# Delta-rule attention and expert layer in one kernel: the second block's norms moved beside tick 0, nineteen inverse steps in ticks 0 to 7, and v's scaling split between ScalarE and VectorE

## The chip, the cores and the metric

The kernel runs on one core of one Trainium2 chip. The metric is device time in microseconds of one execution. Where a trace is quoted, it is of one profiled execution, and times in it count from that execution's first instruction. The engines are named as the profile names them: PE is TensorE (PEld its weight loads), DVE is VectorE, ACT is ScalarE, POOL is GpSimd, SP is the engine that issues most DMAs.

## What is computed

```python
batch, n_heads, seq, head_dim = (4, 8, 768, 48)
k_n = k / (np.linalg.norm(k, axis=-1, keepdims=True) + 1e-06)
state = np.zeros((B, H, D, D))
for t in range(S):
    y[:, :, t] = einsum('bhd,bhde->bhe', q[:, :, t], state)
    v_old = einsum('bhde,bhd->bhe', state, kt)
    state = state + bt[:, :, :, None] * einsum('bhd,bhe->bhde', kt, vt - v_old)
...
x = y.transpose(0, 2, 1, 3).reshape(3072, 384)
# then 8 experts, top 1 by x @ w_gate: out = gate * (relu(x @ w1[e]) @ w2[e])
```

The first part is a recurrence over 768 tokens for 32 pairs of batch and head. The second part sends each of 3072 tokens through one of eight expert networks.

## The kernel before

**Blocks, sub-blocks and ticks.** The 768 tokens are cut into six blocks (`tb`) of 128, and each block into four sub-blocks of 32 tokens. A pair of block and batch has a number n = 4 tb + b, from 0 to 23. The recurrence runs as a pipeline of 27 ticks: in tick t, sub-block q of pair n = t − q is treated for q = 0 to 3, and q sits on partitions 32q to 32q + 31. So a tick works on 128 partitions, and each block takes four more ticks.

**What one tick does, in the order of the code.** `residual(t)` multiplies the keys with the state and with earlier results on PE (the `ks` matmuls of L392 and L404) and subtracts that from the scaled v on DVE (L411, `v_all<-v_all,ks`). `apply(t)` multiplies with the inverse on PE (L419, `ks<-v_all,wt`), and ACT copies the four results out (L423, `u<-ks`). PE can't start L419 of a tick before DVE's L411 of that tick, and DVE can't start L411 before the `ks` matmuls of that tick. Besides, each tick holds a part of `kpart` (transposed keys, and their Gram matrices: matmuls `pg`, ACT copies `gg`, L244), of `qpart` (matmuls `pq`, ACT copies `pm`), of `finish` (state update `st`, output `yp`, router logits) and of `emit_slots`. PE's matmuls `pt`, `qt`, `pg` and `pq` share one ring of three PSUM buffers, six tiles a tick, so that the second half of `pq` takes the buffer that the first `gg` copy frees.

**Norms and inverses of a block.** For each block DVE has two long jobs. `prepare(tb)` finds the norms of the keys from the diagonals of the Gram matrices (`ss<-lg` is its first instruction, then a square root on ACT at L302, then ten short instructions, and the transposes into `nt_all`). `lanes(tb)` inverts 32x32 triangular matrices column by column: 31 columns, each a product (`tmp`, L353) and a difference (`lw`, L360), one generator step each, and at the end a transpose into `wt` (L366), which `apply` uses. The Gram diagonals reach `prepare` through DRAM: when the fourth pair of a block has its `gg` copies, SP issues four writes `gd<-gg` and one read `lg<-gd` (L248, L251). This happens in ticks 2, 6, 10 and 14 for blocks 2 to 5, and before tick 0 for block 1.

**Order.** All instructions of the recurrence stand on each engine in the order of the code. `inverses(steps, t)` takes steps of `prepare` or `lanes` of the next block from a queue, and `beside(t, i)` calls it at seven places of each tick with `STEPS = (3, 3, 3, 2, 2, 2, 2)`, 17 steps a tick. `scale_v(t + 1)` multiplies the next tick's v with the norms, one DVE instruction (L375, 128 x 384). Before tick 0, the kernel runs `prepare(0)`, `scale_v(0)`, 56 steps of `lanes(0)`, all of `prepare(1)` and the rest of `lanes(0)`.

**Experts.** From tick 20 on, weights are loaded and split into two parts, and after tick 26 the experts run, bound by PE.

Of the kernel before, what the change touches and what calls it, by code (L numbers as in the profile page):

```python
# [12 lines left out]
AF = mybir.ActivationFunctionType  # L13
# [5 lines left out]
B, H, S, D = 4, 8, 768, 48  # L19
C = 128  # L20
NT = S // C
# [19 lines left out]
def deltanet_moe(ctx, tc, q, k, v, beta, w_gate, w1, w2, out):  # L41
    nc = tc.nc
# [62 lines left out]
    LAG = NB - 1  # L105
# [2 lines left out]
            -4, -1, 'l')  # L108

    STEPS = (3, 3, 3, 2, 2, 2, 2)  # L110
    W1 = 4
    DM2 = 0
    DEF = 2
# [35 lines left out]
    nt_t = lp.tile([128, (NT * B + LAG) * H], F32, name="nt_all")  # L149
# [38 lines left out]
    def rows(t):  # L188

        if t < NB:  # L190
            return [slice(0, 32 * (t + 1))]
        return {NT * B: [slice(32, 64), slice(64, 128)], NT * B + 1: [slice(64, 128)],
                NT * B + 2: [slice(96, 128)]}.get(t, [slice(0, 128)])
# [91 lines left out]
    def prepare(tb):  # L285

        T = tiles[tb]
        if tb == 0:
            T["lg"] = fp.tile([128, 32, 32], F32, name="lg0", tag="lg", bufs=2)
        lg = T["lg"]  # L290
        lw = T["lw"]
        ss, s0, r0 = (lp.tile([128, 32], F32, name=f"{n_}{tb}", tag=n_) for n_ in ("ss", "s0", "r0"))
        if tb == 0:
            nc.vector.transpose(out=ss, in_=sst)
            yield
            nc.vector.tensor_scalar(out=ss, in0=ss, scalar1=1e-36, scalar2=None, op0=ALU.max)
        else:
            nc.vector.tensor_scalar(out=ss, in0=lg.rearrange("p a b -> p (a b)")[:, 0:1024:33],
                                    scalar1=1e-36, scalar2=None, op0=ALU.max)
        for _ in range(6 if tb > 1 else 1):  # L300
            yield
        nc.scalar.activation(out=s0, in_=ss, func=AF.Sqrt)  # L302
        yield
        nc.vector.reciprocal(r0, s0)
        yield
        nc.vector.tensor_tensor(out=r0, in0=r0, in1=ss, op=ALU.mult)
        yield
        nc.vector.tensor_tensor(out=s0, in0=s0, in1=r0, op=ALU.add)
        yield
        nc.vector.tensor_scalar(out=s0, in0=s0, scalar1=0.5, scalar2=1e-6, op0=ALU.mult, op1=ALU.add)  # L310
        yield
        nc.vector.reciprocal(r0, s0)
        yield
        nc.vector.tensor_tensor(out=ss, in0=r0, in1=bl[:, tb, :], op=ALU.mult)
        yield
        nc.vector.tensor_tensor(out=lw.rearrange("p a b -> p (a b)")[:, 0:1024:33], in0=ss, in1=r0, op=ALU.mult)
        yield
        nc.vector.tensor_tensor(out=r0, in0=ss, in1=r0, op=ALU.mult)
        yield
        if tb == 0:  # L320
            nc.vector.transpose(out=lg, in_=tiles["dg"].rearrange("p h t -> p t h"))
            yield
        nc.vector.tensor_tensor(out=lg, in0=lg, in1=r0.unsqueeze(2).broadcast_to([128, 32, 32]), op=ALU.mult)
        for q in range(NB):
            p = slice(32 * q, 32 * q + 32)
            nc.vector.transpose(out=nt_t[p, (B * tb + q) * H:(B * tb + q) * H + 32], in_=s0[p])
            yield
        T["nt"] = True
# [39 lines left out]
            clear_w(tb + 2)  # L368
        yield

    def scale_v(t):

        vn = vt[t]
        for r in rows(t):
            nc.vector.tensor_tensor(out=vn[r], in0=vn[r], in1=nt_t[r, t * H:(t + 1) * H].unsqueeze(2)  # L375
                                    .broadcast_to([r.stop - r.start, H, D]), op=ALU.mult)

    def clear_u(n):
        us[n] = lp.tile([128, H * D], F32, name=f"u{n}", tag="u", bufs=UB)

        nc.sync.dma_start(out=us[n][32:128], in_=zrow[32:128, 0:H * D])
# [31 lines left out]
    def apply(t):  # L413

        ks, vn = tiles["ks", t], vt[t]
        for h in range(H):
            for q, n in stage(t):
                r = slice(32 * q, 32 * q + 32)
                nc.tensor.matmul(ks[r, h, :], lhsT=tiles[n // B]["wt"][r, n % B * H + h, :], rhs=vn[r, h, :],  # L419
                                 start=True, stop=True, tile_position=(32 * q, 32 * q), skip_group_check=True)  # L420
        for i, (q, n) in enumerate(reversed(stage(t))):
            r = slice(32 * q, 32 * q + 32)
            nc.scalar.copy(out=uview(n)[r], in_=ks[r])  # L423
            if i == 2:
                yield

    def finish(n):
# [29 lines left out]
        yield  # L457
        w = 1 if n >= NN - W1 else 2
        if n % w == 0:
# [97 lines left out]
    def run(gen, steps=1):  # L557

        for _ in range(steps):
            if next(gen, tiles) is tiles:  # L560
                return False
        return True

    def chunk(q, t=-1):

        while q and q[0][0] <= t:
            if run(q[0][1]):
                return
            q.pop(0)
# [154 lines left out]
    NN = NT * B  # L724
# [12 lines left out]
    for i in range(NB):  # L737
        nc.sync.dma_start(out=bl[32 * i:32 * i + 32],
                            in_=beta.rearrange("b h (t i s) -> i (b h) t s", t=NT, i=NB)[i])
# [8 lines left out]
    lane = prepare(0)  # L748
# [15 lines left out]
    slots += [xt[e * CAP + NG * 128:e * CAP + NG * 128 + 64, :].unsqueeze(1) for e in range(E)]  # L764
    while "nt" not in tiles[0]:
        run(lane)
    scale_v(0)
    clear_u(0)
    qs0 = {n: qs_[n][1] for n in range(NN)}
    ks0 = {n: ks_[n][1] for n in range(NN)}  # L770
# [5 lines left out]
    ks_ = [x for i, x in enumerate(ks_) if f"k{i}" not in done]  # L776
    qs_ = [x for i, x in enumerate(qs_) if f"q{i}" not in done]
    lane = lanes(0)
    run(lane, 56)
    run(prepare(1), 100)  # L780
    run(lane, 100)
    queue = [(tb, lanes(tb)) for tb in range(1, NT)]
    before = [(tb, prepare(tb)) for tb in range(2, NT)]
    W = None

    def inverses(steps, t):

        while steps > 0 and queue:
            tb, lane = queue[0]
            if t < B * (tb - 1) and "cols" not in tiles[tb - 1] or ("cols" in tiles[tb] and t < B * tb - 1):  # L790
                break
            if before and before[0][0] == tb:
                if run(before[0][1]):
                    steps -= 1
                else:
                    before.pop(0)
            elif run(lane):
                steps -= 1
            else:
                queue.pop(0)  # L800
# [4 lines left out]
    def ahead_step():  # L805
        if order and not (order[0] == "o" and len(last) < DEF):
            run(other if order.pop(0) in "to" else ahead)

    def beside(t, i):

        inverses(STEPS[i], t)
        if before and (t, i) >= (B * before[0][0] - 5, 3):
            if not run(before[0][1], 3):
                before.pop(0)
        for _ in range(STEPS[i] if t < NN - B else 4):
            if fine and not run(fine[0]):
                fine.pop(0)
        for _ in range(WSL.count((t, i))):
            run(W)
        for _ in range(ES.count((t, i))):  # L820
            ahead_step()

    fin = iter(())
    for t in range(NN + LAG):
        if t < NN and t % B == 0 and t > 0:
            while queue and queue[0][0] <= t // B:
                inverses(1, t)
            if t == NN - B:
                ep_.close()
                wq.append(ep.enter_context(tc.tile_pool(name="wr", bufs=1, side="right")))  # L830
                xq_.append(ep.enter_context(tc.tile_pool(name="xq", bufs=1, side="right")))
                W = pieces()
                run(W)
        residual(t)
        beside(t, 0)
        chunk(ks_, t)
        chunk(qs_, t)
        run(fin)
        if t + 1 < NN + LAG:
            scale_v(t + 1)  # L840
        if t + 1 < NN:
            clear_u(t + 1)
        beside(t, 1)
        copies = apply(t)
        run(copies)
        for tb in range(1, NT):
            for i in range(NB):
                if t == B * (tb - 1) + i:
                    load_v(tb, i)
        fin = finish(t - LAG) if t >= LAG else iter(())  # L850
        run(fin)
        beside(t, 2)
        run(fin)
        run(copies)
        beside(t, 3)
        chunk(ks_, t)
        beside(t, 4)
        run(fin)
        beside(t, 5)
        chunk(qs_, t)  # L860
        beside(t, 6)
        for x in slots[t + 1 if t else 0:t + 2]:
            nc.sync.dma_start(out=x, in_=zrow[0:x.shape[0]].unsqueeze(1).broadcast_to(x.shape))
    i = 0
# [107 lines left out]
    def small(nm, shape=(128, E), dt=F32):  # L972
        return op.tile(list(shape), dt, name=nm)
# [40 lines left out]
    for n0 in range(B * NT):  # L1014
# [3 lines left out]
                                     in_=idc, in_offset=None)  # L1018
    LP = tc.For_i(0, nblk, 1)
    LP.__enter__()  # L1020
    if True:
        ind, sel, t8 = small("ind"), small("sel"), small("t8")
        ei, j0, ce, r, rc, gi, ov = (small(n_, (128, 1)) for n_ in ("ei", "j0", "ce", "r", "rc", "gi", "ov"))
# [66 lines left out]
        for f in range(KF):  # L1090
# [4 lines left out]
                                     in_=yo, in_offset=None, bounds_check=N - 1, oob_is_err=False)  # L1095
# [29 lines left out]
```

## Time and profile before

| | before |
|---|---|
| three runs | 581.86, 583.13, 583.75 us; median 583.13 |
| the profiled execution | 578.27 us |
| its span, first to last instruction | 576.6 us |
| mean granted clock of PE | 0.959 |
| PE busy | 514.3 us, 89% |
| DVE busy | 375.8 us, 65% |
| ACT busy | 266.4 us, 46% |

The span is what the trace covers; 1.67 us of the profiled execution lie around it. The shares are means over the whole kernel. The ticks begin at 48.8 us and end near 315 us, and the experts take the rest.

### The profile page before, as it was taken

How to read it: one execution, taken by the hardware profiler on the slowest of the kernel's cores; microseconds unless marked ns; L12 is line 12 of the kernel's file. 1: busy time of each engine (PE TensorE's matmuls, PEld its weight loads, DVE VectorE, ACT ScalarE, POOL GpSimd, SP SyncE). 2: the span in 40 equal slices, each digit the busy share in tenths (PEclk: the TensorE clock that was granted, in tenths of full speed). 3: DMA queues.
4: the chain of work that ended last, by engine and by line, in shares of the span. 5: the costliest groups of instructions: out<-in, count | busy, mean ns of one | idle time of the engine just before them, and what ended most of it. 6: DMA issues, size and time to landing. Idle time of an engine off the chain costs nothing.

```text
span 576.6 us, 17592 instructions
## 1 busy us (share of the span) xinstructions
PE 514.3 (89%) x7284; PEld 466.6 (81%) x7285; DVE 375.8 (65%) x1372; ACT 266.4 (46%) x506; POOL 97.6 (17%) x122
## 2 busy tenths in 40 slices
PE   7845778998989988998899899999999999999992
PEld 4635667887878877887788899999999999999991
DVE  5798967999989999965843377264453627273311
ACT  2541644655656545467633355253443535353310
POOL 5000110132222302214212110101111010201011
PEclk9785997999999989899999899999999999999997
DMA  9954979978777675575712458364544547371000
GB/s 182 162 110 117 238 166 245 224 166 222 154 181 181 134 178 119 126 225 167 210 58 85 133 156 237 118 179 131 165 134 137 143 123 207 105 201 47 25 17 25
DMA packets 153636, 85.51 MB, mean 148 GB/s; under 512 B 121565, under 2 KB 147534, under 8 KB 153552
## 3 DMA queue, kind: packets, MB, share of 16 engines
q1 hardware_dynamic: 150096, 74.78, 52.3%
q0 software_dynamic: 3456, 9.57, 4.7%
q8 instruction: 58, 0.95, 0.7%
q14 instruction: 26, 0.21, 0.1%
HBM read 54.05 MB, written 24.37 MB: 136 GB/s over the span
## 4 chain that ended last, share of the span: by engine, by line
PE 58%; DVE 23%; DMA 7%; SPq 4%; ACT 3%; issue 3%; POOL 0%; ACTq 0%; DVEq 0%; POOLq 0%
PE h L650 21%; PE y L660 17%; DVE tmp L353 6%; DVE lw L360 6%; PE y L940 4%; DMA gd<-gg 3%; DMA lg<-gd 3%; PE ks L419 2%; DVE wt L366 2%; PE yp L435 2%; DVE v_all L411 2%; SPq L248 1%; PE pg L259 1%; PE xp L476 1%; PE ks L392 1%
## 5 line engine op out<-in xcount | busy, mean ns | idle before, releaser
L660 PE MATMUL y<-w2h,hx 128*128 128x384 f32 x352 | 93.4, 339 | 0.0
L353 DVE TENSOR_TENSOR tmp<-lg,lw 128x84 f32<-128x84 f32 (+26 forms) x372 | 82.8, 263 | 0.3
L583 DVE TENSOR_TENSOR w2l<-w2r,w2h 128x768 fp32r<-128x768 f32 x32 | 31.2, 978 | 74.4 <-ACT w2h L582 74.4
L360 DVE TENSOR_TENSOR lw<-lw,tmp 128x84 f32<-128x84 f32 (+26 forms) x372 | 77.7, 250 | 0.3
L663 POOL DMA_INDIRECT out_dram<-yo,idx x32 | 30.7, 958 | 225.8 <-ACT yo L935 170.2
L660 PEld LDWEIGHTS y<-w2h,hx 128*128 128x128 f32 x352 | 63.8, 188 | 0.9
L423 ACT COPY u<-ks 32x384 f32<-32x384 f32 x96 | 45.2, 470 | 40.2 <-PE ks L419 38.6
L650 PE MATMUL h<-xh,w1h 128*128 128x448 f32 x168 | 61.4, 365 | 0.0
L650 PE MATMUL h<-xh,w1l 128*128 128x448 f32 x168 | 61.3, 365 | 0.0
L650 PE MATMUL h<-xl,w1h 128*128 128x448 f32 x168 | 61.3, 365 | 0.0
L660 PE MATMUL y<-w2l,hx 128*128 128x384 f32 x176 | 59.0, 335 | 0.0
L277 POOL TENSOR_SCALAR_AFFINE_SELECT pm<-pm 128x1024 f32<-128x1024 f32 x24 | 33.0, 1373 | 144.4 <-ACT pm L276 144.3
L419 PE MATMUL ks<-v_all,wt 32*32 32x48 f32 x1536 | 26.1, 207 | 34.4 <-DVE v_all L411 33.0
L419 PEld LDWEIGHTS ks<-v_all,wt 32*32 32x32 f32 x1536 | 21.8, 108 | 39.4 <-DVE v_all L411 36.5
L654 DVE SCALAR_TENSOR_TENSOR hx<-h,hx 128x448 fp32r<-128x448 f32 (+1 forms) x64 | 36.9, 587 | 23.7 <-ACT hx L653 23.4
L653 ACT ACTIVATE hx<-h 128x448 fp32r<-128x448 f32 (+1 forms) x64 | 32.3, 516 | 37.5 <-PE h L650 37.5
L935 ACT ACTIVATE yo<-y,gt 128x384 f32<-128x384 f32 x22 | 12.8, 582 | 74.4 <-PE y L660 60.2
L392 PE MATMUL ks<-st,kt 128*32 128x96 f32 x768 | 43.0, 249 | 0.1
L550 POOL DMA_INDIRECT xg<-row,sli x22 | 23.2, 1055 | 93.8 <-DVE sli L543 58.4
L392 PEld LDWEIGHTS ks<-st,kt 128*32 128x32 f32 x768 | 32.1, 109 | 3.6 <-issue 0.4
L244 ACT COPY gg<-pg 128x512 f32<-128x512 f32 x48 | 25.8, 588 | 18.2 <-PE pg L259 18.0
L583 DVE TENSOR_TENSOR w1l<-w1r,w1h 128x1024 fp32r<-128x1024 f32 x24 | 29.5, 1227 | 7.2 <-ACT w1h L582 6.8
(169 smaller groups left out, 1061.2 us busy)
## 6 DMA issues: line engine op xcount, KB each, us to landing
w1r<-in_moe_w_dram SPq DMA_DIRECT2D x24, 512.0 KB, 3.9
w2r<-in_moe_w_dram SPq DMA_DIRECT2D x32, 384.0 KB, 3.5
xg<-zrow SPq DMA_DIRECT2D x7, 788.0 KB, 7.3
kn<-in_k_dram SPq DMA_DIRECT2D x24, 192.0 KB, 4.9
qn<-in_q_dram SPq DMA_DIRECT2D x24, 192.0 KB, 4.3
xr<-xg SPq DMA_DIRECT2D x7, 591.0 KB, 6.2
xn<-row SPq DMA_DIRECT2D x10, 394.0 KB, 4.9
ku<-in_k_dram SPq DMA_DIRECT2D x20, 192.0 KB, 4.1
```

What stands on the lines that cost most here:

```text
L277: nc.gpsimd.affine_select(out=pm, in_=pm, compare_op=ALU.is_gt, fill=0.0, base=0, pattern=[[0, H], [1, C]], channel_multiplier=-1)
L353: nc.vector.tensor_tensor(out=x, in0=lg[:, r0:r1, c:c + 1].broadcast_to([128, r1 - r0, b - a]), in1=lw[:, c:c + 1, a:b].broadcast_to([128, ...
L360: nc.vector.tensor_tensor(out=lw[:, r0:r1, a:b], in0=lw[:, r0:r1, a:b], in1=x, op=ALU.subtract)
L392: nc.tensor.matmul(ks[32 * q:32 * q + 32, 2 * p:2 * p + 2, :], lhsT=kt_t[n % KSL][:, p, 32 * q:32 * q + 32], rhs=st_view(n % B, p), start= ...
L419: nc.tensor.matmul(ks[r, h, :], lhsT=tiles[n // B]["wt"][r, n % B * H + h, :], rhs=vn[r, h, :], start=True, stop=True, tile_position=(32 * ...
L423: nc.scalar.copy(out=uview(n)[r], in_=ks[r])
L583: nc.vector.tensor_tensor(out=lo, in0=src, in1=hi.bitcast(F32), op=ALU.subtract)
L650: nc.tensor.matmul(ps, lhsT=w[:, d, fs], rhs=x_[:, d], start=(n == 0), stop=(n == len(terms) - 1))
L653: nc.scalar.activation(out=hh, in_=ps, func=AF.Relu)
L654: nc.vector.scalar_tensor_tensor(out=hl, in0=ps, scalar=0.0, in1=hh.bitcast(F32), op0=ALU.max, op1=ALU.subtract)
L660: nc.tensor.matmul(ps, lhsT=h(f)[h_], rhs=w2[w][:, f, :], start=(n == 0), stop=(n == len(terms) - 1))
L663: nc.gpsimd.indirect_dma_start(out=out, out_offset=bass.IndirectOffsetOnAxis(ap=idx, axis=0), in_=yo, in_offset=None, bounds_check=N - 1, ...
```

## The change

Three things change. `prepare(1)` is no longer run before tick 0, but is taken in ticks beside the other work: three steps of it at each `beside` of tick 0 on top of those that `inverses` takes; `prepare(2)` may start in tick 4 at its first place, and `inverses` may start it earlier. `scale_v(0)` stands after 20 steps of `lanes(0)` rather than ahead of them. In ticks 0 to 7, 19 steps of the inverses are taken instead of 17. And in ticks 4 to 19, the scaling of the next tick's v is eight ScalarE activations (one for each head, 128 x 48, with the norm as the scale of each partition), placed after the four `u` copies; in the other ticks it stays one DVE instruction.

```diff
     STEPS = (3, 3, 3, 2, 2, 2, 2)
+
+    STEPS0 = (4, 3, 3, 3, 2, 2, 2)
...
-    def scale_v(t):
+    def scale_v(t, act=False):
...
         vn = vt[t]
         for r in rows(t):
+            for h in range(H if act else 0):
+                nc.scalar.activation(out=vn[r, h], in_=vn[r, h], func=AF.Copy, scale=nt_t[r, t * H + h:t * H + h + 1])
+            if act:
+                continue
             nc.vector.tensor_tensor(out=vn[r], in0=vn[r], in1=nt_t[r, t * H:(t + 1) * H].unsqueeze(2)
                                     .broadcast_to([r.stop - r.start, H, D]), op=ALU.mult)
...
-    scale_v(0)
     clear_u(0)
...
     lane = lanes(0)
-    run(lane, 56)
-    run(prepare(1), 100)
+    run(lane, 20)
+    scale_v(0)
     run(lane, 100)
     queue = [(tb, lanes(tb)) for tb in range(1, NT)]
-    before = [(tb, prepare(tb)) for tb in range(2, NT)]
+    before = [(tb, prepare(tb)) for tb in range(1, NT)]
...
-        inverses(STEPS[i], t)
-        if before and (t, i) >= (B * before[0][0] - 5, 3):
+        inverses((STEPS0 if t < 2 * B else STEPS)[i], t)
+        if before and (t, i) >= ((B, 0) if before[0][0] == 2 else (B * before[0][0] - 5, 3)):
...
-        if t + 1 < NN + LAG:
+        if t + 1 < NN + LAG and not B <= t < NN - B:
             scale_v(t + 1)
...
+
+        if B <= t < NN - B:
+            scale_v(t + 1, act=True)
         beside(t, 3)
```

On PE, SP and POOL the instructions keep their order. On DVE and ACT three places matter. The first is DVE at the start of tick 0, after the transpose `wt` of block 0; `lg_521` and `lw_185` belong to block 1. Before:

```order
L366 STREAM_TRANSPOSE wt_751<-lw_183 128x32x32
L411 TENSOR_TENSOR v_all<-v_all,ks_755 32x384
L353 TENSOR_TENSOR tmp_0_761<-lg_521,lw_185 128x15
L353 TENSOR_TENSOR tmp_0_761<-lg_521,lw_185 128x16
L360 TENSOR_TENSOR lw_185<-lw_185,tmp_0_761 128x15
```

And in the change, where `lg_520` is block 1's:

```order
L368 STREAM_TRANSPOSE wt_733<-lw_183 128x32x32
L417 TENSOR_TENSOR v_all<-v_all,ks_737 32x384
L300 TENSOR_SCALAR ss_743<-lg_520 128x32
L306 RECIPROCAL r_745<-s_744 128x32
L308 TENSOR_TENSOR r_745<-r_745,ss_743 128x32
L310 TENSOR_TENSOR s_744<-s_744,r_745 128x32
L312 TENSOR_SCALAR s_744<-s_744 128x32
L314 RECIPROCAL r_745<-s_744 128x32
L381 TENSOR_TENSOR v_all<-v_all,nt_all 64x384
L316 TENSOR_TENSOR ss_743<-r_745,bl 128x32
```

All of `prepare(1)` stood ahead of the last three columns of block 0, and now stands behind tick 0's subtraction.

The second place is DVE at the end of tick 3, where block 1's inverse ends (`lw_185`, then `wt`) and block 2's norms begin (`ss<-lg` needs the read `lg<-gd` of block 2). Before:

```order
L360 TENSOR_TENSOR lw_185<-lw_185,tmp_30_746 128x19
L298 TENSOR_SCALAR ss_1274<-lg_1101 128x32
L366 STREAM_TRANSPOSE wt_1290<-lw_185 128x32x32
L304 RECIPROCAL r_1276<-s_1275 128x32
L306 TENSOR_TENSOR r_1276<-r_1276,ss_1274 128x32
L308 TENSOR_TENSOR s_1275<-s_1275,r_1276 128x32
```

Seven more rows of `prepare(2)` follow there, and only then tick 4's subtraction L411. In the change:

```order
L362 TENSOR_TENSOR lw_185<-lw_185,tmp_30_1269 128x19
L368 STREAM_TRANSPOSE wt_1286<-lw_185 128x32x32
L300 TENSOR_SCALAR ss_1300<-lg_1096 128x32
L417 TENSOR_TENSOR v_all<-v_all,ks_1318 128x384
L306 RECIPROCAL r_1302<-s_1301 128x32
L308 TENSOR_TENSOR r_1302<-r_1302,ss_1300 128x32
L310 TENSOR_TENSOR s_1301<-s_1301,r_1302 128x32
```

The transpose now stands ahead of the instruction that waits for the read, and the subtraction directly behind it. For blocks 4 and 5 this place keeps its order, and for block 3 only `wt` moves, ahead of the reciprocal.

The third place is ACT in tick 4. Before:

```order
L477 COPY row_0_1388<-xp_0_1390 128x384
L423 COPY u_784<-ks_1329 32x384
L423 COPY u_898<-ks_1329 32x384
L423 COPY u_1034<-ks_1329 32x384
L423 COPY u_1196<-ks_1329 32x384
L244 COPY gg_103<-pg_1_0_1475 128x4x128
L244 COPY gg_103<-pg_1_1_1476 128x4x128
L456 COPY yt_1_1500<-yp_1_1444 128x512
```

In the change, with L378 the new activations:

```order
L483 COPY row_0_1379<-xp_0_1381 128x384
L429 COPY u_768<-ks_1318 32x384
L429 COPY u_886<-ks_1318 32x384
L429 COPY u_1026<-ks_1318 32x384
L429 COPY u_1194<-ks_1318 32x384
L378 ACTIVATE v_all<-v_all,nt_all 128x48 x8
L246 COPY gg_103<-pg_1_0_1472 128x4x128
L246 COPY gg_103<-pg_1_1_1473 128x4x128
L462 COPY yt_1_1497<-yp_1_1433 128x512
```

Eight activations stand between the last `u` copy and the first `gg` copy, in each of the 16 ticks (from tick 15 on, which has no `gg`, ahead of `yt`). DVE's row L375 is gone in those ticks.

## Rows read from the trace of the kernel before

**Rows 1.** Chain that ended last, 46 to 92 us: start, length, what.

```profile
71.30 0.42 SPq L248
...
73.94 4.18 DMA gd<-gg
78.14 4.54 DMA lg<-gd
...
82.89 1.89 DVE wt L366
...
88.25 0.56 DVE v_all L411
```

**Rows 2.** Windows: us; busy PE, PEld, DVE, ACT, POOL; clock, DMA, GB/s.

```profile
57.10:65.60 8.50, 6.88 (x136) 5.95 (x135) 8.50 (x36) 5.24 (x10) 1.67 (x2) 1.00 1.04 253
...
88.30:98.00 9.70, 9.14 (x217) 8.18 (x218) 6.32 (x36) 4.57 (x9) 0.43 (x1) 0.78 0.98 245
...
323.80:576.60 252.80, 241.34 (x1315) 227.60 (x1315) 116.97 (x202) 101.70 (x172) 29.52 (x36) 0.98 0.44 128
```

**Rows 3.** DVE in order of time, up to tick 3; idle before in brackets.

```profile
21.47 0.55 DVE L375 TENSOR_TENSOR v_all<-v_all,nt_all 32x384 f32<-32x384 f32 x1 [2.78 <-DMA v_all<-in_v_dram]
...
40.92 0.18 DVE L298 TENSOR_SCALAR ss<-lg 128x32 f32<-128x32 f32 x1
...
45.54 0.32 DVE L353 TENSOR_TENSOR tmp<-lg,lw 128x36 f32<-128x36 f32 x2
...
48.80 0.52 DVE L411 TENSOR_TENSOR v_all<-v_all,ks 32x384 f32<-32x384 f32 x1
...
57.08 0.55 DVE L411 TENSOR_TENSOR v_all<-v_all,ks 64x384 f32<-64x384 f32 x1 [2.65 <-PE ks L404]
```

**Rows 4.** DVE in order of time, ticks 3 to 8.

```profile
73.63 0.54 DVE L411 TENSOR_TENSOR v_all<-v_all,ks 128x384 f32<-128x384 f32 x1
...
82.70 0.19 DVE L298 TENSOR_SCALAR ss<-lg 128x32 f32<-128x32 f32 x1 [4.57 <-DMA lg<-gd]
...
125.28 0.20 DVE L298 TENSOR_SCALAR ss<-lg 128x32 f32<-128x32 f32 x1 [0.93 <-DMA lg<-gd]
...
130.04 0.56 DVE L411 TENSOR_TENSOR v_all<-v_all,ks 128x384 f32<-128x384 f32 x1
```

**Rows 5.** PE in order of time: first matmuls of ticks 4, 6, 7, 8, 16, 20.

```profile
88.86 1.50 PE L419 MATMUL ks<-v_all,wt 32*32 32x48 f32 x64 [3.64 <-DVE v_all L411]
...
109.71 0.88 PE L419 MATMUL ks<-v_all,wt 32*32 32x48 f32 x64 [0.34 <-DVE v_all L411]
...
119.08 0.88 PE L419 MATMUL ks<-v_all,wt 32*32 32x48 f32 x64
...
130.65 0.88 PE L419 MATMUL ks<-v_all,wt 32*32 32x48 f32 x64 [2.17 <-DVE v_all L411]
...
211.02 0.88 PE L419 MATMUL ks<-v_all,wt 32*32 32x48 f32 x64 [2.51 <-DVE v_all L411]
...
249.02 0.88 PE L419 MATMUL ks<-v_all,wt 32*32 32x48 f32 x64 [0.45 <-DVE v_all L411]
```

**Rows 6.** ACT, DVE and PE in order of time in tick 10.

```profile
151.66 1.96 ACT L423 COPY u<-ks 32x384 f32<-32x384 f32 x4 [0.90 <-PE ks L419]
...
152.24 0.55 DVE L375 TENSOR_TENSOR v_all<-v_all,nt_all 128x384 f32<-128x384 f32 x1
...
154.40 1.07 ACT L244 COPY gg<-pg 128x512 f32<-128x512 f32 x2 [0.78 <-PE pg L259]
...
155.31 1.16 PE L259 MATMUL pq<-qt,kt 64*128 64x128 f32 x16
```

**Rows 7.** ACT in order of time, in the experts.

```profile
338.64 0.58 ACT L935 ACTIVATE yo<-y,gt 128x384 f32<-128x384 f32 x1 [2.03 <-PE y L660]
339.12 0.82 ACT L582 CAST w2h<-w2r 128x768 fp32r<-128x768 f32 x1
```

**Rows 8.** PE in order of time, tick 1.

```profile
60.61 1.16 PE L259 MATMUL pq<-qt,kt 64*128 64x128 f32 x14 [0.45 <-ACT gg L244]
```

## The prediction

> **What bounds the kernel now.** I read the chain of waits first, since it tells which engine's work the end hangs on. In the ticks it runs through one DMA round trip per block: SP writes the Gram blocks from 71.30 us, they land at 78.12, the read back lands at 82.68, DVE's `ss` takes it, and then `wt` (1.89 us) and the norms stand ahead of tick 4's subtraction at 88.25 [rows 1]. The windows by tick come next. In tick 1 DVE is busy for the whole window and the DMA engines are full (1.04); in tick 4 PE is busy for 9.14 of 9.70 us at a mean clock of 0.78 (a mix of its two levels, 1.2 and 2.4 GHz), with the DMA engines at 0.98; and in the 252.8 us of the experts PE is busy for 241.34 [rows 2]. So the experts only follow the end of the ticks, and what the change is worth is decided before 249 us. There, three things are close together: DVE's queue, PE's work in a tick, and the round trips.
>
> **1. Before tick 0.** DVE idles 2.78 us until v has landed, then works through `lanes(0)`; `prepare(1)` takes 45.54 − 40.92 = 4.62 us of it [rows 3]. In the change v's scaling comes after 20 of the 56 steps, some 6 to 7 us of the 19 between the scaling and 40.92, so v is there by then; and `prepare(1)` comes after tick 0's subtraction. That subtraction moves from 48.80 to 48.80 − 2.78 − 4.62 = 41.40. Block 1's read doesn't hold it up: DVE did not wait for it at 40.92, and will ask at about 41.9.
>
> **2. Ticks 0 to 3.** `prepare(1)` is not saved, it moves. In tick 0 DVE did 57.08 − 48.80 − 2.65 = 5.63 us of work and waited 2.65 for PE [rows 3]. Now 4.62 come in and, by the order of rows, about three columns of some 0.68 us (19 us for 28) go to later ticks: about 8.2 us, against the 8.28 that PE took. So PE's slack covers it, and tick 1 begins some 7.4 us earlier. Up to the end of block 1's last column DVE's work is conserved: it ended at 82.70 − 4.57 = 78.13 [rows 4], and now, with `wt` ahead of the wait, at 41.40 + (78.13 − 48.80 − 2.65) + 4.62 + 1.85 = 74.55. The 19 steps only shift columns between the ticks. Tick 3's subtraction stood at 73.63, 4.5 us ahead of that end; with `wt` and one more column behind it, it now stands at 74.55 − 4.5 − 1.85 − 0.65 = 67.55.
>
> The round trip of block 2 hangs on SP's issues and on full DMA engines, which start with the ticks; I let it land 7.3 us earlier, at 75.4. `ss` waits 0.85 us instead of 4.57, and tick 4's subtraction comes directly behind it, at 75.6 instead of 88.25. But then PE is late: tick 3's first matmul starts 0.6 us after the subtraction (88.25 to 88.86), at 68.15, and a tick takes PE 119.08 − 109.71 = 9.37 us without a wait worth naming [rows 5]. So tick 4's matmuls start at 77.55 and not at 76.2. They stood at 88.86: **−11.3**. PE no longer idles 3.64 us ahead of them; that idle was followed by slow matmuls (1.50 us where the other ticks have 0.88), which should go too.
>
> **3. Eight activations on ScalarE.** DVE loses one instruction of 0.55 us (0.5 in its queue) in 16 ticks [rows 6]. ScalarE gains eight. The trace has no activation of this shape. The nearest, with a scale for each partition, takes 0.58 us for 384 columns, and the next starts 0.48 after it [rows 7]. From 384 to 768 columns (0.49 for a `u` copy, 0.82 for a cast) a column costs 0.86 ns, so 336 columns less take 0.29 off: 0.19 in a row, 0.29 alone. Bounds for one: 0.04 (its columns only) and 0.58 (the row as it is). I take 0.20, because the overlap of 0.1 is seen in rows 7: 8 × 0.20 + 0.1 = 1.7 us for the group.
>
> The Trainium skill (ScalarE: Activation LUTs, What ACT_TABLE_LOAD costs) gives such an activation 280 ns and 0.833 ns a column, with 93 ns of overlap, which makes 1.9 us for eight. For 384 columns that is 0.60 us, and rows 7 show 0.58. The sum would be some 2 us worse by it. Its section Rules for kernel authors puts a multiplication on VectorE, not ScalarE; the last rival below is what would follow if that mattered here.
>
> Where it lies: in tick 10 the `u` copies end at 153.62, and the first `gg` copy starts at 154.40 [rows 6]. With the group it starts at 155.32, 0.92 later, and ends its first half at 155.9. `pq` starts at 155.31, and its second half needs the buffer of that copy; that this wait exists is seen in tick 1, where PE stood 0.45 us for it [rows 8]. So PE now stands about 0.55 us in each tick with `gg` copies: 9.95 instead of 9.4. The later ACT work has idle time ahead of it and absorbs the rest.
>
> **4. Ticks 4 to 7.** Two ticks of PE, 77.55 + 19.9 = 97.45 for tick 6 (109.71 before). DVE has about 9 us of work in each and follows. From there the round trip of block 3 sets the pace: 125.28 − 109.71 = 15.57 us [rows 4, 5], and 0.92 for the late `gg`, which feeds the writes: `ss` at 113.9. From `ss` to tick 8's subtraction it was 4.76; `ss` now stands one step later, 4.3. With 0.6 more, tick 8's matmuls start at 118.85 instead of 130.65: **−11.8** so far.
>
> **5. Ticks 8 to 15** take 211.02 − 130.65 = 80.37 us, 10.05 each. DVE's 8 × 0.5 = 4 us can't show, since PE needs 9.95, and the reads of blocks 4 and 5 come 0.92 later each. Bounds: −3.8 (DVE alone counts) and +4 (every delay counts). PE's own tick and the two reads are nearest: **+1.2**.
>
> **6. Ticks 16 to 19** (38.0 us) have no `gg`, PE waits for DVE there (2.51 and 0.45 at the two ends of the stretch), and DVE gives back 4 × 0.5. I count **−1.4**.
>
> Sum: −11.8 + 1.2 − 1.4 = −12.0. The profiled execution would take 578.27 − 12.0 = 566.3 us (its span 564.6); it lay 4.9 below the median of the runs, so the median goes from 583.13 to 571.1. This leans on the moved norms; v's scaling on ScalarE is worth about nothing in it.
>
> **Rivals.** A: the forecast, 50%, by itself 568.5 to 573.5.
>
> B, 15%: the group is short (0.12 an activation or less) or `pq` doesn't wait. Then PE's tick stays at 9.4, tick 8 starts at 116.85 (−13.8), and of DVE's 6 us in ticks 8 to 19 some 3.5 show: 565.8. ScalarE's idle time speaks for it, the 0.48 of rows 7 against.
>
> C, 17%: the round trips don't follow the ticks, since the DMA engines are full anyway [rows 2] and the ticks that they serve get shorter. If block 2's read lands at 82.7 as before, DVE just waits longer at `ss`: tick 4 −5.4, and with 4 to 6 about −6: 577. If only block 3's is 4 us late: 575. Against it: the writes of rows 1 start with SP's issue, and SP issues as the ticks release it.
>
> D, 11%: the activations don't overlap, 0.29 each. The group takes 2.3 us, PE stands 1.1 in each tick, 10.5 in all; tick 8 −10.3, ticks 8 to 15 +3.5, then −1.4: −8, 575.
>
> E, 4%: slower than before. An activation costs as much as the one of rows 7 whatever its width, 0.58. The group takes 4.7 us, PE stands 3.5 us in each of the 11 ticks 4 to 14, and the kernel ends near 600. It turns slower than before from about 3 us for the group, 0.38 an activation. Some 3% more are left for what I don't see.
>
> **The numbers.** 571.1 is the likeliest. The range takes in B, C and D: 565.5 to 577.5. About 0.3%, 1.7 us, is what a measurement of this kernel can tell from no change. All cases but E and the rest are faster by more; a worse C could end within it: faster 0.91, within 0.04, slower 0.05.
>
> **What would show it.** In the profile after: the first subtraction near 41.4; `ss` of block 1 without a wait; tick 4's first matmul near 77.5 without a wait for DVE; eight activations in a row of about 1.7 us; a wait of `pq` for `gg` near 0.5 us in ticks 4 to 14; ticks 8 to 15 about as long as before. Wrong would be a long wait at `ss` of blocks 2 and 3 (C), a group above 2 us (D, E), or ticks of 9.4 us (B).

## The result, and the profile after

The change took 576.82 us, the median of 4 runs (575.21 to 578.43), against 583.44 for the kernel before (581.86 to 584.93): a ratio of 0.9886, with a 95% interval of 0.9837 to 0.9935. Two later comparisons of the same two kernels gave 0.9817 (0.9759 to 0.9875) and 0.9838 (0.9785 to 0.9892). So the change saves 6.6 to 10.7 us by the three ratios; 12.0 were forecast. (The ratios and their intervals leave disturbed runs out, so they need not be the quotient of the medians.)

PE's first matmuls of ticks 0, 1, 2, 4, 6, 8, 12, 16 and 20 in the first profile after (span 575.6 us; L425 is L419 of before), as in [rows 5]: start, length, tile, idle time before in brackets.

```profile
42.69 1.48 PE L425 MATMUL ks<-v_all,wt 32*32 32x48 f32 x16 [7.06 <-DVE v_all L417]
...
52.26 0.87 PE L425 MATMUL ks<-v_all,wt 32*32 32x48 f32 x32
...
60.85 1.50 PE L425 MATMUL ks<-v_all,wt 32*32 32x48 f32 x48 [2.13 <-DVE v_all L417]
...
80.72 0.88 PE L425 MATMUL ks<-v_all,wt 32*32 32x48 f32 x64
...
100.50 0.88 PE L425 MATMUL ks<-v_all,wt 32*32 32x48 f32 x64
...
123.64 0.88 PE L425 MATMUL ks<-v_all,wt 32*32 32x48 f32 x64 [3.12 <-DVE v_all L417]
...
166.17 1.26 PE L425 MATMUL ks<-v_all,wt 32*32 32x48 f32 x64 [1.97 <-DVE v_all L417]
...
208.31 1.50 PE L425 MATMUL ks<-v_all,wt 32*32 32x48 f32 x64 [3.60 <-DVE v_all L417]
...
245.67 0.88 PE L425 MATMUL ks<-v_all,wt 32*32 32x48 f32 x64 [0.21 <-DVE v_all L417]
```

Tick 4 starts 8.1 us earlier than in [rows 5] and without its wait, tick 8 7.0, tick 16 2.7, tick 20 3.4. PE waits 2.13 us ahead of tick 2, and the matmuls behind that wait take 1.50 us. A wait was there before too, but the matmuls behind it took 0.88 (1.36 in a second profile). Tick 2 of the kernel before:

```profile
66.24 0.88 PE L419 MATMUL ks<-v_all,wt 32*32 32x48 f32 x48 [1.80 <-DVE v_all L411]
```

DVE in the same profile, around the first subtraction and at block 3's read (as in [rows 3, 4]):

```profile
40.34 1.91 DVE L368 STREAM_TRANSPOSE wt<-lw 128x1024 f32<-128x1024 f32 x1
42.12 0.51 DVE L417 TENSOR_TENSOR v_all<-v_all,ks 32x384 f32<-32x384 f32 x1
42.57 0.15 DVE L300 TENSOR_SCALAR ss<-lg 128x32 f32<-128x32 f32 x1
...
118.02 0.19 DVE L300 TENSOR_SCALAR ss<-lg 128x32 f32<-128x32 f32 x1 [2.82 <-DMA lg<-gd]
```

The first subtraction stands at 42.12 (41.4 was forecast), block 1's `ss` directly behind it without a wait, and block 3's `ss` waits 2.82 us for its read where it waited 0.93 in [rows 4]. That longer wait is not the change's: a second profile of the kernel before, taken at the end of the experiments, has 2.56 there.

The chain of waits of the same profile in tick 4: start, length, what.

```profile
83.13 0.47 ACT u L429
83.60 1.81 ACT v_all L378 x8
85.41 0.47 ACT gg L246
85.88 0.04 issue
85.93 1.16 PE pq L261 x14
```

The eight activations stand on the path, between the last `u` copy and `gg`, as step 3 had it. What that costs PE shows in the 16 matmuls of `pq`, which took 1.16 us before [rows 6]. In tick 5 of the change:

```profile
95.19 1.74 PE L261 MATMUL pq<-qt,kt 64*128 64x128 f32 x16
```

So the wait for the buffer that the first `gg` copy frees, forecast at 0.55 us, is there with 0.58. It lies between the matmuls of the row, so that the row shows no idle time ahead of it. Nine of the eleven ticks 4 to 14 have it; ticks 8 and 12 have 0.20 and nothing. ACT by groups and shapes, where the profile gives the mean of one in ns behind the busy time:

```profile
L378 ACT ACTIVATE v_all<-v_all,nt_all 128x48 f32<-128x48 f32 x128 | 30.5, 319 | 0.0
```

One takes 0.319 us, a group 1.91 from its first start to its last end (in the chain 1.81, since `gg` begins before the last has ended). I had taken 0.29 alone and 1.7 for the group. The Trainium skill (ScalarE: Activation LUTs, What ACT_TABLE_LOAD costs) gives 280 ns and 0.833 ns a column, which makes, as an estimate, 0.32 us for one and, with its overlap, 1.9 for eight: the rows agree with it.

The windows of the profile after: ticks 0 to 3, tick 2 alone, ticks 4 to 7, 8 to 15, tick 16 alone, ticks 16 to 19, 20 to 25, the experts (columns as in [rows 2]).

```profile
42.70:80.70 38.00, 34.92 (x616) 31.24 (x616) 34.38 (x154) 19.38 (x39) 4.84 (x4) 0.76 0.87 207
60.80:71.50 10.70, 10.40 (x170) 9.33 (x171) 9.80 (x46) 3.84 (x8) 1.36 (x1) 0.53 0.77 138
80.70:123.60 42.90, 39.37 (x937) 34.65 (x936) 36.69 (x177) 31.15 (x83) 7.55 (x6) 1.00 0.89 214
...
123.60:208.30 84.70, 77.49 (x1848) 68.56 (x1848) 69.05 (x357) 61.09 (x163) 16.64 (x16) 0.97 0.70 164
...
208.30:245.70 37.40, 34.00 (x860) 30.31 (x861) 35.04 (x173) 24.87 (x70) 8.42 (x8) 0.92 0.48 120
208.30:218.60 10.30, 10.29 (x212) 9.30 (x212) 8.80 (x51) 5.94 (x16) 2.55 (x3) 0.71 0.42 114
245.70:308.90 63.20, 55.79 (x1150) 50.33 (x1150) 35.55 (x110) 33.97 (x70) 13.48 (x12) 1.00 0.53 161
322.80:575.60 252.80, 241.33 (x1316) 227.61 (x1315) 117.04 (x202) 101.55 (x172) 29.53 (x36) 0.98 0.44 128
```

The experts take the same 252.8 us as in [rows 2]. Tick 2 ran almost wholly at the lower of PE's two levels (mean 0.53 of 2.4 GHz), after the 2.13 us idle; tick 16, after 3.60 us, at a mean of 0.71; but tick 8, after 3.12 us, at 1.00. Tick 2 of the kernel before, after its 1.80 us, ran at 1.00 too (0.79 in the second profile of that kernel):

```profile
65.60:73.60 8.00, 6.01 (x168) 5.25 (x168) 8.00 (x37) 4.43 (x9) 1.73 (x1) 1.00 1.03 221
```

### The profile page after: what moved, and what is told of

Its sections match the earlier page's. It is cut to its first block, busy times and chain, and to the rows that moved or that the text cites. A ratio compares the mean times of both kernels' runs of the same rounds, so it can differ in the third digit from the quotient of the medians.

```text
span 575.6 us, 17719 instructions
## 1 busy us (share of the span) xinstructions
PE 523.0 (91%) x7285; PEld 473.4 (82%) x7285; DVE 367.8 (64%) x1356; ACT 291.9 (51%) x634; POOL 92.4 (16%) x122
## 4 chain that ended last, share of the span: by engine, by line
PE 68%; DVE 13%; ACT 7%; DMA 6%; issue 2%; SPq 1%; POOL 0%; DVEq 0%; POOLq 0%; ACTq 0%
PE h L656 21%; PE y L666 17%; DVE lw L362 4%; PE y L948 4%; DVE tmp L355 4%; PE ks L425 3%; PE pq L261 3%; PE ks L398 3%; ACT v_all L378 3%; ACT u L429 2%; PE xp L482 2%; PE yp L441 2%; PE yp L459 2%; PE ks L410 2%; PE pt L219 2%
## 5 line engine op out<-in xcount | busy, mean ns | idle before, releaser
L362 DVE TENSOR_TENSOR lw<-lw,tmp 128x84 f32<-128x84 f32 (+26 forms) x372 | 79.4, 254 | 0.3
L355 DVE TENSOR_TENSOR tmp<-lg,lw 128x84 f32<-128x84 f32 (+26 forms) x372 | 78.0, 250 | 0.3
L279 POOL TENSOR_SCALAR_AFFINE_SELECT pm<-pm 128x1024 f32<-128x1024 f32 x24 | 27.8, 1158 | 154.5 <-ACT pm L278 154.5
L943 ACT ACTIVATE yo<-y,gt 128x384 f32<-128x384 f32 x22 | 12.8, 581 | 74.7 <-PE y L666 60.2
L425 PE MATMUL ks<-v_all,wt 32*32 32x48 f32 x1536 | 27.3, 211 | 23.8 <-DVE v_all L417 23.0
L425 PEld LDWEIGHTS ks<-v_all,wt 32*32 32x32 f32 x1536 | 22.8, 111 | 28.4 <-DVE v_all L417 25.1
L398 PE MATMUL ks<-st,kt 128*32 128x96 f32 x768 | 44.8, 255 | 0.4 <-issue 0.4
L261 PE MATMUL pq<-qt,kt 64*128 64x128 f32 x384 | 35.8, 300 | 2.0 <-ACT gg L246 0.9
L398 PEld LDWEIGHTS ks<-st,kt 128*32 128x32 f32 x768 | 33.4, 112 | 3.5 <-issue 0.6
L261 PEld LDWEIGHTS pq<-qt,kt 64*128 64x128 f32 x384 | 29.1, 198 | 8.5 <-issue 4.7
```

Of the source, the lines that this page charges most:

```text
L261: nc.tensor.matmul(pg[a][:, p], lhsT=kt[r, p], rhs=xt[r, p], start=True, stop=True, tile_position=(64 * a, 0), skip_group_check=True)
L355: nc.vector.tensor_tensor(out=x, in0=lg[:, r0:r1, c:c + 1].broadcast_to([128, r1 - r0, b - a]), in1=lw[:, c:c + 1, a:b].broadcast_to([128, ...
L362: nc.vector.tensor_tensor(out=lw[:, r0:r1, a:b], in0=lw[:, r0:r1, a:b], in1=x, op=ALU.subtract)
L398: nc.tensor.matmul(ks[32 * q:32 * q + 32, 2 * p:2 * p + 2, :], lhsT=kt_t[n % KSL][:, p, 32 * q:32 * q + 32], rhs=st_view(n % B, p), start= ...
```

## The experiments

Theory P, from these rows: the moved norms are worth 9 to 10 us, and the group of activations gives 3 to 4 back. Rival R: the group is free, and the shortfall lies in the clock and in ticks 20 to 26. The first four kernels tell them apart.

**The change again, beside the others.** No edit.

> The changed kernel again, beside the three others. Both theories: 576.8 us, ratio 0.989 to the kernel before. Theory P says that this is the sum of two effects: the moved norms take about 9 to 10 us off, and the ScalarE group ahead of the gg copies gives 3 to 4 back (pq stands about 0.5 us for gg in ticks 4 to 14, the reads of the Gram blocks come later by 1.2 to 1.9). Theory R says that the group costs nothing, and that the norms alone are worth only 6 to 7, since the slower PE clock of tick 2 and the scatters of ticks 20 to 26 take the rest.

Measured: 572.0 us (median; lowest to highest 570.3 to 576.5), ratio to the kernel before 0.9817 (95% interval 0.9759 to 0.9875). The other results stand in the same order.

**Norms and steps only**, v's scaling on DVE in all ticks:

```diff
-        if t + 1 < NN + LAG and not B <= t < NN - B:
+        if t + 1 < NN + LAG:
             scale_v(t + 1)
...
-        if B <= t < NN - B:
-            scale_v(t + 1, act=True)
```

> Norms and 19 steps as in the change, v's scaling on VectorE in all ticks as before. P: 573 us (ratio 0.982), 3 to 4 us faster than the change; PE's tick between ticks 4 and 6 is 9.4 us instead of 9.9, gg follows the u copies with no group between, and the clock in ticks 12 and 16 is no lower than before. R: 577 to 580 us, as the change or slower by what DVE's 0.5 us in 16 ticks brings (at most 3); ticks 8 to 16 stay near 84.7 us or get longer.

Measured: 576.0 us (573.4 to 580.4), 0.9883 (0.9825 to 0.9940): not faster than the change, where P had it 3 to 4 us faster. P falls. Of PE's waits from 80 to 208 us (total, times, longest), first in the change, then in this kernel:

```profile
PE ks L425 <- DVE v_all L417: 5.1, 2, 3.1
```

```profile
PE ks L425 <- DVE v_all L417: 8.0, 7, 2.4
```

Without the group, PE waits for DVE seven times instead of twice (three times, 7.2 us, in the second profile of the change). `pq` takes 1.16 us again, but ticks 4 to 6 take 31.2 us (tick 4 at 80.1, tick 7 at 111.3) against 29.6 in the change (80.7 to 110.3): DVE is busy for 29.4 of the 31.2, and PE idles 2.5 of them against 0.3 in the change. So in these ticks the group's delay takes the place of another, most likely DVE's: the profile names DVE for 1.1 of the 2.5, and no engine for the rest.

**ScalarE's group only**, in the kernel before, with its norms and steps (`scale_v` has the `act` branch of the change, not shown here):

```diff
-        if t + 1 < NN + LAG:
+        if t + 1 < NN + LAG and not B <= t < NN - B:
             scale_v(t + 1)
...
+        if B <= t < NN - B:
+            scale_v(t + 1, act=True)
```

> The kernel before, with v's scaling as eight ScalarE activations in ticks 4 to 19 as the only edit. P: 586 to 587 us (ratio 1.005 to 1.007), ticks 8 to 16 longer than 80.4 us by 3 or more, less what ticks 16 to 20 give back. R: 580 to 583 us (ratio 0.995 to 1.000).

Measured: 582.8 us (577.8 to 586.8), 0.9999 (0.9964 to 1.0034). R's forecast. By itself the group is worth nothing that the interval of some 2 us either way can show.

**The group behind the `gg` copies:**

```diff
+        beside(t, 3)
+        chunk(ks_, t)
         if B <= t < NN - B:
             scale_v(t + 1, act=True)
-        beside(t, 3)
-        chunk(ks_, t)
```

> The change, with the eight activations moved behind the two gg copies of the same tick on ScalarE: DVE's relief stays, and gg and the Gram blocks' writes are no later than before. P: 572 to 573 us (ratio 0.98 to 0.982), no wait of pq for gg, and the reads come 15.6 to 15.9 us after their tick's first matmul as before. R: 577 us as the change, or slower, if the work behind the group (yt, pm) or tick t+1's subtraction then waits for it.

Measured: 575.7 us (574.6 to 578.5), 0.9862 (0.9812 to 0.9912): as the change. In its profile ticks 4 to 6 are shorter (29.0 us), but block 3's read then comes 20.1 us after tick 6's first matmuls (98.1 to 118.27), and tick 8 starts at 124.7. There `pq` takes 1.16 us, so moving the group takes the wait away, and the total is no better for it: the place of the group makes no difference that these runs can show. That leaves two readings. Q: the group is on the path, but DVE's 0.55 us stood there just as much. S: ScalarE's idle time hides it.

**A second group behind the first**, to a tile that nobody reads; the output is the same:

```diff
             if act:
+                sc = lp.tile([128, H, D], F32, name=f"sc{t}", tag="sc", bufs=1)
+                for h in range(H):
+                    nc.scalar.activation(out=sc[r, h], in_=vn[r, h], func=AF.Copy, scale=nt_t[r, t * H + h:t * H + h + 1])
                 continue
```

> The change, with a second group of eight such activations right behind the first in ticks 4 to 19 (same input and scale, written to a spare tile that nobody reads; the output stays the same). Theory Q: the group stands on the path in ticks 4 to 14 through gg and pq, and costs nothing in the sum only because VectorE's 0.5 us per tick would stand there otherwise. Then 1.8 us more per tick show almost whole in those 11 ticks, less the little that is slack: 585 to 592 us, ticks of 11.3 us or more, a wait of pq for gg of some 2 us. Rival S: ScalarE's idle time hides the group: at most 4 us more than the change, 572 to 580 us.

Measured: 598.9 us (598.5 to 600.6), 1.0295 (1.0258 to 1.0333). S falls, and Q holds in what this kernel can show, that the group is on the path; the price is above Q's range. PE's wait of `pq` for `gg` from 80 to 230 us (total, times, longest) comes in all eleven ticks 4 to 14:

```profile
PE pq L261 <- ACT gg L246: 21.5, 11, 2.0
```

PE in this kernel's tick 7, and the windows of tick 7 and of ticks 16 to 19:

```profile
126.02 1.16 PE L261 MATMUL pq<-qt,kt 64*128 64x128 f32 x14 [1.93 <-ACT gg L246]
...
129.76 1.09 PE L219 MATMUL pt<-ident,kn 128*128 128x128 f32 x4
130.64 0.84 PE L271 MATMUL qt<-ident,qn 128*128 128x128 f32 x4
```

```profile
119.00:132.30 13.30, 11.37 (x239) 10.13 (x238) 10.96 (x44) 9.87 (x30) 2.07 (x2) 0.87 0.69 186
232.70:268.50 35.80, 33.51 (x860) 29.53 (x862) 34.84 (x175) 30.85 (x101) 7.75 (x8) 0.95 0.44 107
```

The tick takes 13.3 us instead of some 9.9: 1.9 are the wait of `pq`, and about 1.5 more come because the matmuls behind it run for a stretch at the lower clock (`pt` 1.09 us where this kernel's tick 5 has 0.64). Ticks 16 to 19, which have no `gg`, lose nothing: 35.8 us.

**The norms in their old place**, all else as in the change:

```diff
     run(lane, 20)
     scale_v(0)
+    run(lane, 36)
+    run(prepare(1), 100)
     run(lane, 100)
     queue = [(tb, lanes(tb)) for tb in range(1, NT)]
-    before = [(tb, prepare(tb)) for tb in range(1, NT)]
+    before = [(tb, prepare(tb)) for tb in range(2, NT)]
```

> The change, with block 1's norms back ahead of tick 0 (VectorE, 4.6 us); v's scaling still behind 20 steps, 19 steps in ticks 0 to 7, ScalarE's group as in the change. Theory N: the norms' place is worth about 4 to 5 us and the rest comes from v's scaling no longer waiting for v: 577 to 579 us, tick 0 at 46 to 47, tick 4 at 84 to 86. Rival: PE and not VectorE sets ticks 0 to 3 once tick 2 runs at the lower clock, so the place is worth little: 573 to 576 us, with the time before tick 0 made good by shorter ticks 0 to 3.

Measured: 581.7 us (578.2 to 582.8), 0.9999 (0.9975 to 1.0023): the whole gain is gone. Both forecasts were too low. PE's first matmuls of ticks 0 and 4 in its profile:

```profile
47.06 1.17 PE L425 MATMUL ks<-v_all,wt 32*32 32x48 f32 x12 [8.44 <-DVE v_all L417]
...
84.79 0.54 PE L425 MATMUL ks<-v_all,wt 32*32 32x48 f32 x30
```

What is left of the change starts tick 0 2.3 us earlier than before (49.4), and tick 4 4.1 earlier (88.86 in [rows 5]); at the end nothing is left of it. In its profile ticks 8 to 15 take 84.4 us, and ticks 20 to 25 63.4. Where the 4.1 us go is not shown.

**17 steps instead of 19:**

```diff
-    STEPS0 = (4, 3, 3, 3, 2, 2, 2)
+    STEPS0 = (3, 3, 3, 2, 2, 2, 2)
```

> The change, with the old 17 inverse steps in ticks 0 to 7 in place of 19. Prediction's view (the steps only shift columns between ticks, their sum is done when it is done): within 1.5 us of the change, 571 to 577 us. Rival: the 8 fewer steps in ticks 0 to 3 leave 3 us or so of block 1's columns to be done in front of tick 4's subtraction, and block 2's norms behind them: tick 4 later by 2 to 4 us, 576 to 580 us.

Measured: 575.0 us (570.5 to 577.9), 0.9894 (0.9855 to 0.9933): the prediction's view holds for the total. First matmuls of ticks 2, 3, 4 and 8 in its profile:

```profile
58.20 0.88 PE L425 MATMUL ks<-v_all,wt 32*32 32x48 f32 x48 [1.03 <-DVE v_all L417]
...
66.77 0.88 PE L425 MATMUL ks<-v_all,wt 32*32 32x48 f32 x64 [1.85 <-DVE v_all L417]
...
77.53 0.54 PE L425 MATMUL ks<-v_all,wt 32*32 32x48 f32 x30
...
122.54 1.21 PE L425 MATMUL ks<-v_all,wt 32*32 32x48 f32 x60 [4.50 <-DVE v_all L417]
```

Tick 4 starts where step 2 had put it (77.5), with 1.03 us of idle ahead of tick 2 and a clock of 1.00 in it (tick 3, behind 1.85 us, has a mean of 0.84 and takes 10.8 us); but block 2's columns are then not done when block 3's read comes, and PE stands 4.50 us ahead of tick 8.

**ScalarE's group only in ticks 16 to 19:**

```diff
-        if t + 1 < NN + LAG and not B <= t < NN - B:
+        if t + 1 < NN + LAG and not NN - 2 * B <= t < NN - B:
...
-        if B <= t < NN - B:
+        if NN - 2 * B <= t < NN - B:
```

> Norms and steps as in the change, ScalarE's group only in ticks 16 to 19, which have no gg copies; VectorE scales in all others. Theory Q: ticks 4 to 15 as with the scaling on VectorE (no stall of pq, ticks of about 10.1 us), ticks 16 to 19 as in the change, about 1 us shorter than with VectorE: as the change or up to 1.5 us faster, 571 to 575 us. Rival (the relief of VectorE in ticks 4 to 15 is what made the change faster than the kernel with the norms alone, 572.0 against 576.0): 575 to 577 us.

Measured: 571.3 us (567.6 to 575.0), 0.9825 (0.9779 to 0.9871): within Q's range, below the rival's, and not apart from the change.

**The same with 17 steps, and with 17 in ticks 0 to 3 and 19 in ticks 4 to 7**, beside the change. The second one's edit, besides that of the group:

```diff
-        inverses((STEPS0 if t < 2 * B else STEPS)[i], t)
+        inverses((STEPS0 if B <= t < 2 * B else STEPS)[i], t)
```

> Norms moved as in the change, 17 inverse steps as before the change, ScalarE's group only in ticks 16 to 19: the two edits that the runs so far charge with a cost are taken out. If the group costs 1 to 3 us in ticks 4 to 15 and gives 1 to 2 in ticks 16 to 19, and the 19 steps are worth nothing: 569 to 573 us, faster than the change by 1 to 5 on this chip. Rival (all these versions are alike and differ by the scatter of their runs alone): within 1 us of the change of this call.

Measured: 576.2 us (571.7 to 580.6), 0.9846 (0.9796 to 0.9895): not the 569 to 573 us expected. By the ratios it lies within 1 us of the change in the same comparison (0.9838, below), as the rival had it.

> As the kernel just before, with 17 steps in ticks 0 to 3 and 19 in ticks 4 to 7. If the 8 early steps only crowd VectorE in ticks 0 to 2 (its profile with 17 steps starts tick 3 at 66.8 us where 19 steps start it at 70.0 to 71.5) while the later 8 help block 2's columns ahead of tick 8: 568 to 572 us, tick 4 near 77.5 and tick 8 below 122. Rival: as the kernel with 17 steps in all ticks, within 1 us.

Measured: 572.0 us (568.3 to 574.8), 0.9804 (0.9756 to 0.9852). Tick 4 stands at 79.2 and tick 8 at 122.4 in its profile, both later than expected.

> The changed kernel a third time, beside the two above: 571 to 577 us, as its ten runs so far (median 575.1). Its profile is a third execution: if the time from tick 20 to tick 26 and the length of ticks 8 to 15 belong to the change, they are again 62 to 63 and 82 to 85 us; if they are the scatter of executions, they move by 1 to 3 us.

Measured: 573.6 us (570.5 to 578.3), 0.9838 (0.9785 to 0.9892). The second variant, with 17 and 19 steps, has the lowest ratio of all, but its interval and the change's overlap for the most part: no version is shown to beat the change.

**The kernel before, profiled once more.**

> The kernel before, profiled once more, since its one profile lay 4.9 us below the median of its runs. If the places that the change is charged with (ticks 20 to 26 at 60.9 us, ticks 8 to 15 at 80.4) are steady in this kernel, they are the same within 0.7 us and the 4 to 5 us lie elsewhere, most likely ahead of tick 8; if they are scatter, ticks 20 to 26 take 62 or more here too.

Measured: 585.6 us, a span of 583.9. Windows of ticks 4 to 7, 8 to 15, 16 to 19 and 20 to 25, here and in the third profile of the change:

```profile
88.00:132.30 44.30, 40.42 (x939) 36.13 (x939) 35.84 (x173) 24.34 (x50) 7.56 (x6) 0.92 0.85 204
132.30:215.90 83.60, 78.03 (x1848) 69.76 (x1848) 75.53 (x367) 48.34 (x99) 19.56 (x16) 0.94 0.72 169
215.90:254.20 38.30, 34.31 (x858) 30.48 (x858) 37.38 (x179) 18.11 (x37) 9.49 (x8) 0.91 0.47 114
254.20:315.70 61.50, 55.81 (x1151) 50.26 (x1150) 34.23 (x109) 34.21 (x70) 13.44 (x12) 1.00 0.54 165
```

```profile
78.90:121.40 42.50, 39.14 (x937) 34.69 (x936) 36.63 (x177) 31.26 (x83) 7.56 (x6) 1.00 0.91 215
121.40:205.20 83.80, 77.14 (x1852) 68.45 (x1855) 70.17 (x357) 61.28 (x163) 16.66 (x16) 0.98 0.71 169
205.20:242.70 37.50, 34.05 (x858) 30.28 (x858) 35.02 (x173) 24.88 (x70) 8.57 (x8) 0.92 0.49 119
242.70:306.10 63.40, 55.96 (x1151) 50.37 (x1151) 35.82 (x111) 34.09 (x70) 13.63 (x12) 1.00 0.52 160
```

In the kernel before, ticks 4 to 7 took 41.8 us in one profile and 44.3 in the other, ticks 8 to 15 80.4 and 83.6 at clocks of 1.00 and 0.94. So part of what the first profile seemed to charge to the change is scatter.

## Why the prediction was right, and where it was off

All profiles of the two kernels, by stage, in us (stages begin at a tick's first matmul; the forecast's column is the prediction's sum):

| stage | before, 2 profiles | change, 3 profiles | difference of means | forecast |
|---|---|---|---|---|
| up to tick 0 | 49.4, 48.7 | 42.7, 42.0, 42.6 | -6.6 | -7.4 |
| ticks 0 to 3 | 39.5, 39.3 | 38.0, 37.3, 36.3 | -2.2 | -3.9 |
| ticks 4 to 7 | 41.8, 44.3 | 42.9, 42.5, 42.5 | -0.4 | -0.5 |
| ticks 8 to 15 | 80.4, 83.6 | 84.7, 81.8, 83.7 | +1.4 | +1.2 |
| ticks 16 to 19 | 38.0, 38.3 | 37.4, 37.3, 37.5 | -0.8 | -1.4 |
| ticks 20 to 25 | 60.9, 61.5 | 63.3, 62.3, 63.4 | +1.8 | 0 |
| the rest | 266.7, 268.2 | 266.7, 267.8, 266.7 | -0.4 | 0 |
| span | 576.6, 583.9 | 575.6, 570.9, 572.8 | -7.1 | -12.0 |

The mechanism was right in the main: the norms' move is the gain (putting them back took all of it away), v's scaling on ScalarE is worth nothing that can be measured, and the forecast's main term, the time up to tick 4, is there for the greater part. By the profiles the sum was some 5 us too large. That the first result, 576.8, still lay in the range, 0.7 us inside its upper end, is in part luck: cases C and D had set that end, and most of the missing 5 us come from terms that are in neither. The terms:

- **Step 1** held: the first subtraction stood at 42.12, 41.38 and 42.01 in the three profiles, for 41.40; of the 7.4 some 0.8 are missing, part of it because the second profile of before begins tick 0 0.7 us earlier than the first.
- **Step 2 is the term that was mis-sized: of the 3.9 us that ticks 0 to 3 were to save, 2.2 came** (with step 1, -11.3 at tick 4 measured -8.8). Tick 3's matmuls were to start at 68.15 and started at 71.5, 70.0 and 69.7. From there PE is full, and tick 3 takes its 9.24 us (9.37 forecast); so the loss lies in ticks 0 to 2. Two things failed. One is the sentence "The 19 steps only shift columns between the ticks". In tick 2 DVE was full before (8.00 of 8.00 us), and with more columns it is busy for 9.2 to 9.7; each column taken there puts off tick 3, where PE sets the pace and DVE has time left (busy for 7.3 to 7.7 of 9.24 us). The three kernels with 17 steps start tick 3 at 66.8, 67.2 and 68.4; the seven profiles with the norms moved and 19 steps at 69.4 to 71.5, with tick 0 at 42.0 to 42.7 in all ten. The other is that the step took PE's clock as it was in one profile. The extra work of tick 0 was to hide behind "the 8.28 that PE took"; PE is busy for 9.3, 10.5 and 8.2 us of that tick, at mean clocks of 0.59, 0.52 and 0.72, and in the second profile of before it is 9.3 at 0.59 as well. Tick 2's clock is 0.53, 0.63 and 0.63 where the two profiles of before have 1.00 and 0.79. How the loss divides between columns and clock stays open. Nor is the sum shown to be better with 17 steps: PE then stands 4.50 us ahead of tick 8, which starts at 122.5, where the change has 121.4 to 123.6.
- **Step 3**: the group took 1.91 us for 1.7, `pq`'s wait is 0.58 us for 0.55, and PE's tick is 9.84 to 9.94 us from tick 4 to the start of tick 7 (9.95 forecast). What I had wrong is what it displaces. I added the stall to a tick of 9.37, but in the three kernels with the moved norms and the scaling on DVE these ticks take 10.1 to 11.0 us. That case B is out and that this price is real, the doubled group shows; that it nets to about zero, the group alone in the kernel before (0.9999, within 0.35%).
- **Step 4**: the length of ticks 4 to 7 came out. Block 3's read came 17.5, 17.3 and 17.2 us after tick 6's first matmuls, not 16.5. I had read 15.57 off one profile; the second of the kernel before has 16.8, with 5.54 us for SP's four issues of the Gram blocks' writes where the first has 3.05 and the change 4.66 to 5.21. Two kernels without the group there have 16.3 and 18.2. So neither case C nor a cost of the group is shown in it.
- **Step 5** came out (+1.4 for +1.2), inside a scatter of 3 us in either kernel, so the agreement says little. Over all kernels, ticks 8 to 15 take 80.3 to 84.7 us in six profiles without the group there and 80.9 to 84.7 in six with the single group ahead of `gg`: its cost in these ticks is not resolved.
- **Step 6** measured -0.8 for -1.4. In all ten profiles that have the single group there, ticks 16 to 19 take 36.3 to 37.5 us, against 38.0 to 38.3 in the three that scale on DVE. Here the Trainium skill's advice (ScalarE: Activation LUTs, Rules for kernel authors: multiplication on VectorE) doesn't pay: in the kernel before, DVE is busy for 37.1 of 38.0 us in these ticks and ACT for 18.5.
- **Ticks 20 to 25** were put at nothing in the sum, and took 1.8 back, as much as step 2 lacked. Two kernels with the moved norms have 60.2 and 61.1 there (17 steps; the group in ticks 16 to 19 alone), and the group alone, with the norms in their old place, has 62.2, so it isn't tied to the norms. Its cause stays open, and with two profiles of before it may be scatter in part.

## What to carry to other kernels

Where several engines are each nearly full, moving work off one of them is worth only the gap to the next: here eight small activations that stood on the path cost about as much as the VectorE instruction they replaced, and doubling them showed that they were not free. Work moved beside a loop's first rounds has to fit round by round, not in their sum. An idle of 2 to 3 us on TensorE can be followed by slower matmuls, and a range should have room for that, but the length of the idle alone didn't tell: 2.13 us were followed by a mean clock of 0.53 in the tick behind, 1.80 by 1.00 and by 0.79, 3.12 by 1.00, 3.60 by 0.71. One profile of a kernel whose runs scatter by 1% is too little to size a term of 2 us: take two of the kernel before.

## What was not expected of the hardware

An idle of 1.93 us on PE was followed, in the kernel with the doubled group, by matmuls at the lower clock within the same tick, so that a wait of 1.9 us made the tick 3.4 us longer; tick 5 of that kernel, with a wait of 1.90, kept a clock of 1.00. And the same program's runs on one chip differ by 1% (570.3 to 576.5 us for the change), and the three profiles of the change show granted clocks of 0.76, 0.77 and 0.84 in ticks 0 to 3 alone.
